# Transposing q and k together, splitting them in transposed form, and leaving two heads' probabilities unsplit

## The chip, the core and the metric

The kernel runs on one core of one Trainium2 chip. The core has a matrix engine (PE), a vector engine (VectorE, DVE in the rows), a scalar engine (ScalarE, ACT), a general engine (GpSimd, POOL) and a queue that issues transfers (SyncE, SP). Each runs its own instructions in the order written and waits for others by semaphores. PE multiplies a stationary operand, which it loads first (PEld), with a moving one, and writes to PSUM; the others work on on-chip memory, SBUF, and all but GpSimd also on PSUM. The metric is the time of one execution on the device, in microseconds.

## The reference

Two batches of eight heads attend over 768 positions of 64 features, and a position sees only those that fall in its hash bucket. The 1536 rows that come out go through two gated networks.

```python
q_bits = (np.einsum('bhsd,dk->bhsk', q, proj) > 0)     # 6 bits
k_bits = (np.einsum('bhsd,dk->bhsk', k, proj) > 0)
mask = q_bucket[:, :, :, None] == k_bucket[:, :, None, :]
scores = scale * np.matmul(q, k.transpose(0, 1, 3, 2))
scores = np.where(mask, scores, -1000000000.0)
attn = np.exp(scores - np.max(scores, axis=-1, keepdims=True))
attn = attn / (np.sum(attn, axis=-1, keepdims=True) + 1e-09)
return np.matmul(attn, v)
...
h = (x @ w1) * (x @ w2) @ w3                            # first network, then @ w_out
gate = 1.0 / (1.0 + np.exp(-(x @ w_gate)))              # second network
return (gate * (x @ w_val) @ w_out2)
```

The networks' weights come as 64-bit floats.

## The kernel before, in words

**Split operands.** A matmul takes its operands as float32r, a shortened float32 that PE runs in one pass. To keep precision a value is split in two such tiles, a high half (the value copied into float32r) and a low half (the value less its high half), and a product is summed from two or three matmuls. A transpose is a matmul with an identity as moving operand: `idf` in float32, `idr` in float32r.

**Heads.** `load_head` loads q, k and v of a head. `split` makes the split tiles `spq`, `spk`, `spv`: VectorE for heads 0 and 1 (of v only the high half), GpSimd for the later ones. `prep(h)` readies a head: 6 transposes of the split q and 6 of the split k, three into a PSUM tile `trr`; ScalarE copies these to `aq` and `ak` (64 rows of high half, 64 of low half, times 768); the hash `gps` multiplies `aq` and `ak` with the split projection `pq` in 8 matmuls of 384 columns; VectorE turns the signs into large numbers `ft`, which add to the scores what a mismatch costs. Five copies on SP bring the halves into the rows where the score matmul wants them. `first_head` does this for head 0 without those copies.

**Steps.** A head has six steps of 128 query rows, 96 in all. In one, `emit_qk` runs 4 score matmuls of 384 columns into one of two PSUM tiles, VectorE takes the maximum (L479) and a scale (L480), ScalarE the exponential with its sum (L490), PE transposes the probabilities `e` in 6 float32 transposes (L523), ScalarE copies them out as the high half (L526), VectorE writes the low half (L527). For each pair of steps `emit_av` multiplies them with the split v: 6 blocks of 128 keys, each with the high and the low half, 12 matmuls of 256 columns (L540). The stationary operand is the 64 columns of v's high half beside the 64 of its low half, so the result has 128 rows, of which `emit_x` adds the two halves.

**Beside it** runs a filler: 64-bit weights are decoded (`decode`, two ScalarE, one GpSimd and three VectorE instructions each), and w3 and w_out are multiplied into one matrix (`wacc`). From about step 52 the filler is the first network's first chunk of tokens (`gen_first`). After the last head come the networks for the rest (`moe`).

**The order** on each engine is worked out by `order_engines`: it takes all instructions of the attention part with their dependencies and priorities (by step; the preparation of a head 300 earlier), plays them against estimated costs, always starting the ready instruction of the smallest number on a free engine, and ties each engine to the order so found. Its cost of a PE instruction is `n / 2.4` ns for n columns, doubled for a float32 transpose, plus 2.5; of a GpSimd one `60 + n * 2.3`.

Of the kernel before, what the change touches and what calls it, by code (L numbers as in the profile page):

```python
# [228 lines left out]
def lsh_attention_moe_moe2_kernel(  # L229
# [132 lines left out]
    def split(h, nm, part):  # L362
        if not 0 <= h < NH:
            return
        if part == 0:
            t = ap_.tile([P, NT, 2, D], F32R, tag="sp" + nm, name=f"sp{nm}{h}", bufs=2 if nm == "v" else 1)
            splits[h, nm] = t
            (pool if h >= 2 else dve).tensor_copy(t[:, :, 0, :], raws[h, nm])
        else:
            t = splits[h, nm]  # L370
            (dve if h < 2 and nm != "v" else pool).tensor_tensor(out=t[:, :, 1, :], in0=raws[h, nm], in1=f(t[:, :, 0, :]), op=ALU.subtract)

    def alloc_mats(h):
# [4 lines left out]
        mats[h] = m

    def prep(h):  # L380

        load_head(h, "v")
        if h < NH:
            alloc_mats(h)
            m = mats[h]
            for nm, d in (("q", "aq"), ("k", "ak")):
                t = splits[h, nm]
                for half in range(2):
                    ps = psT.tile([P, 512], F32R, tag="t", name="trr")
                    for c in range(3):  # L390
                        pe.transpose(ps[:, c * P:(c + 1) * P], t[:, half * 3 + c].rearrange("p a d -> p (a d)"), idr)  # L391
                    act.activation(out=m[d][:, half * HS:(half + 1) * HS], in_=f(ps[:, :HS]), func=AF.Copy,
                                   scale=SCALE if nm == "q" else 1.0)
                    if nm == "q" and half == 1:
                        sync.dma_start(out=f(m["bq"][0:D]), in_=f(m["aq"][0:D]))
                    yield
            sync.dma_start(out=f(m["bk"][0:D]), in_=f(m["ak"][D:P]))
            for half in range(2):
                hs = slice(half * HS, (half + 1) * HS)
                ps = psT.tile([P, 512], F32, tag="t", name="gps")  # L400
                for n, nm in enumerate(("aq", "ak")):
                    for x in range(2):
                        pe.matmul(ps[:, :HS], lhsT=pq[n][x], rhs=m[nm][:, hs], start=n + x == 0, stop=n + x == 2)  # L403
                dve.tensor_scalar(out=m["ft"][:, hs], in0=ps[:, :HS], scalar1=thr[:, 0:1], scalar2=thr[:, 1:2],
# [11 lines left out]
        split(h - 1, "v", 0)
        split(h - 1, "v", 1)

    def first_head():
# [4 lines left out]
        kt = m["ft"]  # L424
        kps = []
        for nm, d in (("q", m["aq"]), ("k", kt)):
            t = splits[0, nm]
            for half in range(2):
                ps = psT.tile([P, 512], F32R, tag="t", name="trr")
                for c in range(3):  # L430
                    pe.transpose(ps[:, c * P:(c + 1) * P], t[:, half * 3 + c].rearrange("p a d -> p (a d)"), idr)
                kps = (kps + [ps])[-2:]
                act.activation(out=d[:, half * HS:(half + 1) * HS], in_=f(ps[:, :HS]), func=AF.Copy, scale=SCALE if nm == "q" else 1.0)
            if nm == "q":
                pool.tensor_copy(m["bq"][0:D], f(m["aq"][0:D]))
        for half in range(2):
            hs = slice(half * HS, (half + 1) * HS)
            act.activation(out=m["ak"][0:D, hs], in_=f(kps[half][0:D, :HS]), func=AF.Copy)
            dve.tensor_copy(m["ak"][D:P, hs], f(kps[half][0:D, :HS]))
        for half in range(2):  # L440
            act.activation(out=m["bk"][0:D, half * HS:(half + 1) * HS], in_=f(kps[half][D:P, :HS]), func=AF.Copy)
# [1 line left out]
        pss = []
        for half in range(2):
            hs = slice(half * HS, (half + 1) * HS)
            ps = psT.tile([P, 512], F32, tag="t", name="gps")
            pss.append(ps)
# [486 lines left out]
```

## Time and profile before

| | |
|---|---|
| median of 3 runs | 836.71 us (836.36 to 836.72) |
| the profiled execution | 834.55 us |
| its span, first to last instruction | 832.6 us |
| mean granted PE clock | 0.994 of full speed |
| busy: PE, VectorE, ScalarE, GpSimd | 801.0, 540.7, 523.9, 332.0 us |
| chain that ended last | PE 84%, VectorE 8%, ScalarE 5% |

A share of busy time is an average over stages with different limits: the attention part takes somewhat under the first half of the span, the networks the rest. A PE instruction is recorded from its start to its end, while the next starts before that, so PE's busy time says when PE had nothing at all, and the spacing of starts says what an instruction costs.

### The profile page before, as it was taken

What the parts mean: (1) busy time and instruction counts of PE and PEld (TensorE: products, weight loads), DVE (VectorE), ACT (ScalarE), POOL (GpSimd) and SP (SyncE); (2) the same over time, 40 slices, a digit from 0 to 9 for tenths busy, and PEclk for the clock granted to TensorE, in tenths of its full rate; (3) what the DMA queues carried; (4) which work ended last, traced back from release to release, by engine and by line L of the source; (5) the groups of instructions that cost most, each with busy time, mean ns of one, the idle gap of its engine ahead of it and who ended that gap; (6) DMA issues with size and microseconds to landing.
All of it is one profiled execution on the core that took longest, in us unless ns stands there. A gap on an engine that the chain in (4) does not pass through costs nothing.

```text
span 832.6 us, 12204 instructions
## 1 busy us (share of the span) xinstructions
PE 801.0 (96%) x4272; PEld 683.6 (82%) x4272; DVE 540.7 (65%) x969; ACT 523.9 (63%) x1024; POOL 332.0 (40%) x329
## 2 busy tenths in 40 slices
PE   6889989999989999999999999999999999999998
PEld 5767878888878989888888888888888888888886
DVE  7999998888799989988265545586752222222222
ACT  5888977777888998887345555756545333343332
POOL 3466332242355443328534343544443232333330
PEclk9999999999999999999999999999999999999999
DMA  7656554334245543412012122334301000010001
GB/s 236 172 162 170 155 159 134 103 87 130 64 133 136 138 121 99 125 45 77 0 34 94 55 73 93 110 104 150 102 1 51 1 1 1 1 51 1 0 1 50
DMA packets 44748, 71.15 MB, mean 85 GB/s; under 512 B 6096, under 2 KB 32720, under 8 KB 44688
## 3 DMA queue, kind: packets, MB, share of 16 engines
q1 hardware_dynamic: 44688, 70.39, 29.0%
q8 instruction: 33, 0.54, 0.3%
q14 instruction: 27, 0.22, 0.1%
HBM read 52.43 MB, written 3.19 MB: 67 GB/s over the span
## 4 chain that ended last, share of the span: by engine, by line
PE 84%; DVE 8%; ACT 5%; issue 1%; DMA 1%; POOL 0%; SPq 0%; ACTq 0%; DVEq 0%; POOLq 0%
PE m L701 17%; PE pb L701 17%; PE pa L701 17%; PE av L540 6%; PE tp L523 5%; PE p L701 5%; PE wacc L596 4%; PE s L469 3%; PE s L472 3%; PE y L701 3%; PE gps L403 2%; DVE pt L527 2%; DVE s L479 1%; PE trr L391 1%; ACT pt L526 1%
## 5 line engine op out<-in xcount | busy, mean ns | idle before, releaser
L741 DVE TENSOR_TENSOR pb<-pb,a 128x512 f32<-128x512 f32 x52 | 36.2, 698 | 147.1 <-PE pb L701 139.8
L523 PE MATMUL tp<-idf,e 128*128 128x128 f32 x576 | 102.9, 277 | 5.5 <-DVE pt L527 4.3
L490 ACT ACTIVATE e<-s,sm 128x768 f32<-128x768 f32 x96 | 95.8, 998 | 15.7 <-DVE sm L480 15.1
L527 DVE TENSOR_TENSOR pt<-tp,pt 128x384 fp32r<-128x384 f32 x192 | 101.2, 549 | 6.0 <-ACT pt L526 4.4
L336 POOL TENSOR_SCALAR da<-da 128x512 f32<-128x512 f32 x76 | 51.3, 676 | 133.0 <-ACT da L334 119.3
L526 ACT ACTIVATE pt<-tp 128x384 fp32r<-128x384 f32 x192 | 90.4, 494 | 21.4 <-PE tp L523 19.5
L701 PE MATMUL pa<-x,wah 128*128 128x512 f32 x320 | 99.0, 389 | 0.0
L479 DVE TENSOR_REDUCE s<-s 128x1 f32<-128x768 f32 x96 | 91.8, 956 | 11.0 <-PE s L472 10.7
L701 PE MATMUL pb<-x,wbh 128*128 128x512 f32 x320 | 98.5, 389 | 0.0
L695 POOL TENSOR_TENSOR wal<-xall,wah 128x512 fp32r<-128x512 f32 x36 | 47.4, 1317 | 110.2 <-ACT wah L276 109.6
L523 PEld LDWEIGHTS tp<-idf,e 128*128 128x128 f32 x576 | 72.0, 142 | 17.6 <-DVE pt L527 6.0
L540 PE MATMUL av<-pt,spv 128*128 128x256 f32 x576 | 78.7, 287 | 1.0 <-DVE pt L527 0.9
L334 ACT ACTIVATE da<-st 128x512 f32<-128x512 f32 x76 | 51.1, 672 | 42.7 <-DVE w1r L343 18.1
L540 PEld LDWEIGHTS av<-pt,spv 128*128 128x128 f32 x576 | 72.1, 191 | 4.2 <-DVE pt L527 1.3
L469 PE MATMUL s<-ak,aq 128*128 128x384 f32 x192 | 61.8, 386 | 10.7 <-ACT e L490 10.6
L701 PEld LDWEIGHTS pb<-x,wbh 128*128 128x128 f32 x320 | 60.1, 188 | 12.5
L701 PEld LDWEIGHTS pa<-x,wah 128*128 128x128 f32 x320 | 60.1, 188 | 12.5
L596 PE MATMUL wacc<-wo,t 128*128 128x512 f32 x192 | 65.3, 416 | 0.1
L701 PE MATMUL pa<-x,wal 128*128 128x512 f32 x160 | 62.3, 389 | 0.0
L701 PE MATMUL pb<-x,wbl 128*128 128x512 f32 x160 | 62.2, 389 | 0.0
L744 DVE TENSOR_TENSOR gl<-pb,gh 128x512 fp32r<-128x512 f32 x52 | 36.0, 691 | 40.0 <-ACT gh L276 40.0
L472 PE MATMUL s<-bk,bq 128*128 128x384 f32 x192 | 57.2, 359 | 0.3 <-DVE bq L453 0.3
(161 smaller groups left out, 1889.6 us busy)
## 6 DMA issues: line engine op xcount, KB each, us to landing
st<-in_moe_w_dram SPq DMA_DIRECT2D x32, 512.0 KB, 3.8
st<-in_moe_w_out_dram SPq DMA_DIRECT2D x20, 512.0 KB, 3.4
st<-in_moe_w_gate_dram SPq DMA_DIRECT2D x12, 512.0 KB, 3.5
st<-in_moe_w_val_dram SPq DMA_DIRECT2D x12, 512.0 KB, 3.5
rawq<-in_q_dram SPq DMA_DIRECT2D x16, 192.0 KB, 3.4
rawk<-in_k_dram SPq DMA_DIRECT2D x16, 192.0 KB, 3.2
rawv<-in_v_dram SPq DMA_DIRECT2D x16, 192.0 KB, 3.1
rr<-row SPq DMA_DIRECT2D x16, 192.0 KB, 3.3
```

The lines of the kernel that those rows point to most:

```text
L334: act.activation(out=f(a), in_=f(hw), func=AF.Abs)
L336: pool.tensor_scalar(out=f(a), in0=f(a), scalar1=F64_HI, scalar2=F64_LO, op0=ALU.min, op1=ALU.max)
L469: pe.matmul(s[:, half, :HS], lhsT=m["aq"][:, qs], rhs=m["ak"][:, ks], start=True, stop=False)
L472: pe.matmul(s[:, half, :HS], lhsT=m["bq"][:, qs], rhs=m["bk"][:, ks], start=False, stop=True)
L479: dve.tensor_reduce(out=one[:, 1:2], in_=s[:, :, :HS], op=ALU.max, axis=AX.XY, negate=True)
L490: act.activation(out=e.rearrange("p (a c) -> p a c", a=2), in_=s[:, :, :HS], func=AF.Exp, bias=sm[:, 1:2], scale=sm[:, 0:1], accum_out=su_ ...
L523: pe.transpose(ps[:, j * P:(j + 1) * P], e[:, c * P:(c + 1) * P], idf)
L526: act.activation(out=dh, in_=src, func=AF.Copy)
L527: dve.tensor_tensor(out=lo[:, g % 2, half * 3:half * 3 + 3], in0=src, in1=f(dh), op=ALU.subtract)
L540: pe.matmul(acc[:, :2 * P].rearrange("p (a t) -> p a t", a=2), lhsT=w, rhs=r[:, :, c], start=(c == 0 and i == 0), stop=(c == NT - 1 and i ...
L596: pe.matmul(acc, lhsT=t3[x][:, j], rhs=wo[y][:, j], start=(j == 0 and n == 0), stop=(j == NF1 - 1 and n == 2))
L701: mm = pe.matmul(ps, lhsT=lhs[x], rhs=rhs[y], start=start and n == 0, stop=stop and n == 2)
```

## The change

q and k of a head are joined side by side in float32 (`join`; q is scaled there), and one set of 6 float32 transposes turns both: 64 rows of q over 64 of k. ScalarE copies this out whole (`rt`), and the split follows in transposed form: GpSimd casts it into `aq` and subtracts into `bq`. The hash takes three matmuls for a half in place of four: high with high, low with high, high with low, q and k in one. The rows are brought in place by six copies instead of five. In the first two heads (`PLAIN`) the transposed probabilities stay one float32 tile, v is used as loaded, and a product has 6 matmuls on 64 columns of v; VectorE's L527 and L550 fall away there. The two halves of the score product change places. The planner's cost of a PE instruction gets a case of four passes for float32 operands with other than 128 columns.

```diff
-            return n / 2.4 * (2 if n == 128 and "float32r" not in str(rd[0].dtype) else 1) + 2.5
+            passes = 1 if "float32r" in str(rd[0].dtype) else 2 if n == 128 else 4
+            return n / 2.4 * passes + 2.5
...
-            (pool if h >= 2 else dve).tensor_copy(t[:, :, 0, :], raws[h, nm])
-        else:
-            t = splits[h, nm]
-            (dve if h < 2 and nm != "v" else pool).tensor_tensor(out=t[:, :, 1, :], in0=raws[h, nm], in1=f(t[:, :, 0, :]), op=ALU.subtract)
+        raws[h] = t = ap_.tile([P, NT, 2, D], F32, tag="qk", name=f"qk{h}", bufs=1)
+        eng = pool if h else dve
+        eng.tensor_scalar(out=t[:, :, 0, :], in0=raws[h, "q"], scalar1=0.0, scalar2=SCALE, op0=ALU.add, op1=ALU.mult)
+        eng.tensor_copy(t[:, :, 1, :], raws[h, "k"])
...
+    def both(h, half):
+        ps = psT.tile([P, 512], F32, tag="t", name="trr")
+        for c in range(3):
+            pe.transpose(ps[:, c * P:(c + 1) * P], raws[h][:, half * 3 + c].rearrange("p a d -> p (a d)"), idf)
+        return ps[:, :HS]
+    def hashes(m, half):
+        hs = slice(half * HS, (half + 1) * HS)
+        ps = psT.tile([P, 512], F32, tag="t", name="gps")
+        for n, (w, x) in enumerate(((0, "aq"), (0, "bq"), (1, "aq"))):
+            pe.matmul(ps[:, :HS], lhsT=pq[w], rhs=m[x][:, hs], start=n == 0, stop=n == 2)
+        return ps
...
             for half in range(2):
                 hs = slice(half * HS, (half + 1) * HS)
+                act_copy(t[:, hs], both(h, half))
+                pool.tensor_copy(m["aq"][:, hs], t[:, hs])
+                pool.tensor_tensor(out=m["bq"][:, hs], in0=t[:, hs], in1=f(m["aq"][:, hs]), op=ALU.subtract)
+                yield
+            for d in ("ak", "bk"):
+                sync.dma_start(out=f(m[d][0:D]), in_=f(m["aq"][D:P]))
+            sync.dma_start(out=f(m["bk"][D:P]), in_=f(m["bq"][D:P]))
...
+            sync.dma_start(out=f(m["bq"][D:P]), in_=f(m["aq"][0:D]))
+            sync.dma_start(out=f(m["ak"][D:P]), in_=f(m["ft"][0:D]))
+            sync.dma_start(out=f(m["aq"][D:P]), in_=f(m["ft"][D:P]))
             yield
...
-            pt_t[g // 2] = [ap_.tile([P, 2, NT, P], F32R, tag=f"pt{i}", name=f"pt{i}_{g}") for i in range(2)]
+            n, dt = (1, F32) if g < PLAIN * NT else (2, F32R)
+            pt_t[g // 2] = [ap_.tile([P, 2, NT, P], dt, tag=f"pt{i}", name=f"pt{i}_{g}") for i in range(n)]
...
         act.activation(out=dh, in_=src, func=AF.Copy)
-        dve.tensor_tensor(out=lo[:, g % 2, half * 3:half * 3 + 3], in0=src, in1=f(dh), op=ALU.subtract)
+        for d in dl:
+            dve.tensor_tensor(out=d, in0=src, in1=f(dh), op=ALU.subtract)
...
-        act_copy(x, acc[D:P, :2 * P])
-        dve.tensor_tensor(out=x, in0=acc[0:D, :2 * P], in1=x, op=ALU.add)
+        if h < PLAIN:
+            act_copy(x, acc[0:D, :2 * P])
+        else:
+            act_copy(x, acc[D:P, :2 * P])
+            dve.tensor_tensor(out=x, in0=acc[0:D, :2 * P], in1=x, op=ALU.add)
```

The planner's order, at three places. A number behind a name counts buffers; in `e2` or `sm3` the first number is the step, in `spq2` or `aq2` the head.

VectorE in head 0, steps 1 to 5, before (`pt1` is the low half, `da` and `wor` are decoded weights):

```order
L527 TENSOR_TENSOR pt1_0_322<-tp1_344,pt0_0_321 128x384
L527 TENSOR_TENSOR pt1_0_322<-tp1_350,pt0_0_321 128x384
L480 SCALAR_TENSOR_TENSOR sm3_339<-lim_77,s1_84 128x2
L343 ISA wor0_264<-da_370,dr_371 128x1024
L527 TENSOR_TENSOR pt1_2_386<-tp2_387,pt0_2_385 128x384
L527 TENSOR_TENSOR pt1_2_386<-tp2_393,pt0_2_385 128x384
L584 TENSOR_TENSOR t31_0_299<-w3t0_360,t30_0_298 128x512
L479 TENSOR_REDUCE s0_83<-s0_83 128x1
L479 TENSOR_REDUCE s1_84<-s1_84 128x1
L480 SCALAR_TENSOR_TENSOR sm4_380<-lim_77,s0_83 128x2
L527 TENSOR_TENSOR pt1_2_386<-tp3_433,pt0_2_385 128x384
L527 TENSOR_TENSOR pt1_2_386<-tp3_439,pt0_2_385 128x384
```

and now:

```order
L479 TENSOR_REDUCE s0_80<-s0_80 128x1
L338 SCALAR_TENSOR_TENSOR da_255<-st_239,da_255 128x512
L337 TENSOR_SCALAR da_330<-da_330 128x512
L343 ISA w3f_90<-da_255,dr_256 128x1024
L338 SCALAR_TENSOR_TENSOR da_330<-st_241,da_330 128x512
L480 SCALAR_TENSOR_TENSOR sm4_340<-lim_74,s0_80 128x2
L479 TENSOR_REDUCE s1_81<-s1_81 128x1
L343 ISA wor0_229<-da_330,dr_331 128x1024
L480 SCALAR_TENSOR_TENSOR sm5_382<-lim_74,s1_81 128x2
L337 TENSOR_SCALAR da_437<-da_437 128x512
L338 SCALAR_TENSOR_TENSOR da_437<-st_243,da_437 128x512
L343 ISA wor1_230<-da_437,dr_438 128x1024
```

The six low-half rows are gone, and decoding stands where they stood.

PE around the first product of head 0 and the preparation of head 2, before:

```order
L523 MATMUL tp2_393<-idf_69,e2_319 128x128 x3
L391 MATMUL trr_410<-idr_70,spq2_237 128x128 x3
L391 MATMUL trr_415<-idr_70,spq2_237 128x128 x3
L469 MATMUL s1_84<-ak0_135,aq0_133 128x384 x2
L472 MATMUL s1_84<-bk0_136,bq0_134 128x384 x2
L523 MATMUL tp3_433<-idf_69,e3_342 128x128 x3
L523 MATMUL tp3_439<-idf_69,e3_342 128x128 x3
L540 MATMUL av0_445<-pt0_0_321,spv0_247 128x256
L540 MATMUL av0_445<-pt1_0_322,spv0_247 128x256
L540 MATMUL av0_445<-pt0_0_321,spv0_247 128x256
L540 MATMUL av0_445<-pt1_0_322,spv0_247 128x256
L540 MATMUL av0_445<-pt0_0_321,spv0_247 128x256
```

and now (`av0` is the product, `gps` the hash):

```order
L394 MATMUL trr_368<-idf_69,qk2_208 128x128 x3
L523 MATMUL tp2_351<-idf_69,e2_284 128x128 x2
L584 MATMUL w3t0_320<-idf_69,w3f_90 128x128 x3
L394 MATMUL trr_375<-idf_69,qk2_208 128x128 x3
L523 MATMUL tp3_394<-idf_69,e3_304 128x128 x3
L523 MATMUL tp3_399<-idf_69,e3_304 128x128 x3
L541 MATMUL av0_404<-pt0_0_286,spv0_122 64x256 x6
L402 MATMUL gps_419<-aq2_362,pq0_71 128x384
L402 MATMUL gps_419<-bq2_363,pq0_71 128x384
L402 MATMUL gps_419<-aq2_362,pq1_72 128x384
```

One row of six unsplit matmuls stands for twelve, and the hash, which reads the cast `aq2` and the difference `bq2`, now follows the product.

GpSimd in the preparation of heads 2 and 3, before:

```order
L368 CAST spq2_237<-rawq2_189 128x6x64
L371 TENSOR_TENSOR spq2_237<-rawq2_189,spq2_237 128x6x64
L368 CAST spk2_240<-rawk2_191 128x6x64
L371 TENSOR_TENSOR spk2_240<-rawk2_191,spk2_240 128x6x64
L336 TENSOR_SCALAR da_370<-da_370 128x512
L336 TENSOR_SCALAR da_479<-da_479 128x512
L371 TENSOR_TENSOR spv1_664<-rawv1_193,spv1_664 128x6x64
L368 CAST spq3_654<-rawq3_243 128x6x64
L591 TENSOR_TENSOR wo1_92<-wor0_264,wo0_91 128x512
L371 TENSOR_TENSOR spq3_654<-rawq3_243,spq3_654 128x6x64
```

and now:

```order
L374 TENSOR_SCALAR qk2_208<-rawq2_166 128x6x64
L375 COPY qk2_208<-rawk2_168 128x6x64
L336 TENSOR_SCALAR da_255<-da_255 128x512
L336 TENSOR_SCALAR da_330<-da_330 128x512
L336 TENSOR_SCALAR da_437<-da_437 128x512
L417 CAST aq2_362<-rt2_367 128x384
L418 TENSOR_TENSOR bq2_363<-rt2_367,aq2_362 128x384
L417 CAST aq2_362<-rt2_367 128x384
L418 TENSOR_TENSOR bq2_363<-rt2_367,aq2_362 128x384
L374 TENSOR_SCALAR qk3_468<-rawq3_211 128x6x64
L375 COPY qk3_468<-rawk3_213 128x6x64
```

The split rows that read loaded data become rows that read `rt`, the transposed pair, with the two joining rows of the next head behind them.

## Rows read from the trace of the kernel before

**Rows 1.** The page's forty equal slices, PE and VectorE, busy tenths in order of time.
```profile
PE   6889989999989999999999999999999999999998
DVE  7999998888799989988265545586752222222222
```

**Rows 2.** Busy us by engine (instructions) in four stages, clock, DMA share, GB/s.
```profile
14.00:83.00 69.00, 58.86 (x373) 50.72 (x372) 66.52 (x124) 60.18 (x126) 40.73 (x44) 0.95 0.64 176
83.00:215.00 132.00, 125.78 (x836) 111.84 (x836) 117.02 (x222) 102.19 (x215) 40.54 (x49) 1.00 0.45 122
250.00:385.00 135.00, 134.76 (x883) 120.31 (x884) 119.90 (x237) 115.06 (x244) 56.85 (x62) 1.00 0.42 114
385.00:832.60 447.60, 443.79 (x1958) 367.18 (x1957) 196.55 (x296) 210.75 (x367) 170.56 (x145) 1.00 0.14 45
```

**Rows 3.** The chain of waits within 14 to 83 us, its shares by line.
```profile
by line: DVE pt L527 16.7%; issue 8.9%; DVE da L338 8.3%; DVE s L479 7.9%; DVE wor L343 5.7%; ACT pt L526 5.4%; DMA st<-in_moe_w_dram 4.6%; ACT wo L276 4.3%; PE gps L403 4.1%; ACT e L490 3.6%; ACT da L334 2.9%; DVE da L337 2.6%; DVE sm L480
```

**Rows 4.** Groups of instructions in 14 to 83 us: count, busy us, mean ns, idle before.
```profile
L527 DVE TENSOR_TENSOR pt<-tp,pt 128x384 fp32r<-128x384 f32 x34 | 18.2, 548 | 1.4 <-ACT pt L526 1.2
L550 DVE TENSOR_TENSOR xall<-av,xall 64x256 f32<-64x256 f32 x7 | 2.9, 413 | 0.1
L371 DVE TENSOR_TENSOR spk<-rawk,spk 128x384 fp32r<-128x384 f32 x1 | 0.6, 555 | 0.0
L368 DVE CAST spv<-rawv 128x384 fp32r<-128x384 f32 x1 | 0.4, 357 | 0.0
L392 ACT ACTIVATE ak<-trr 128x384 fp32r<-128x384 f32 x8 | 3.7, 495 | 0.1
L392 ACT ACTIVATE aq<-trr 128x384 fp32r<-128x384 f32 x8 | 3.6, 492 | 0.5 <-PE trr L391 0.5
L523 PE MATMUL tp<-idf,e 128*128 128x128 f32 x106 | 18.9, 284 | 2.0 <-DVE pt L527 1.7 <-DVE xall L550 0.2
L368 POOL CAST spq<-rawq 128x384 fp32r<-128x384 f32 x4 | 3.4, 844 | 8.9 <-PE trr L391 4.7 <-DMA rawq<-in_q_dram 4.2
```

**Rows 5.** The chain of waits within 222 to 240 us: start, us, what, then its last piece.
```profile
222.35 1.38 PE av L540 x12
223.73 0.21 PE trr L391 x3
228.13 0.69 PE gps L403 x4
228.82 0.33 PE tp L523 x3
229.15 0.36 PE s L472 x2
...
823.35 5.45 PE m L701 x24
```

**Rows 6.** Busy us by engine in a busy stretch of heads 1 to 3.
```profile
60.00:100.00 40.00, 37.35 (x250) 32.13 (x249) 39.65 (x77) 36.42 (x77) 21.20 (x24) 1.00 0.60 165
```

**Rows 7.** Groups of GpSimd instructions over the whole run.
```profile
L371 POOL TENSOR_TENSOR spq<-rawq,spq 128x384 fp32r<-128x384 f32 x14 | 16.1, 1152 | 1.0
L368 POOL CAST spq<-rawq 128x384 fp32r<-128x384 f32 x14 | 9.8, 697 | 12.4 <-PE trr L391 8.2 <-DMA rawq<-in_q_dram 4.2
```

**Rows 8.** Instructions in order of time around the start: start, us, what, idle before.
```profile
13.65 0.22 DVE L480 SCALAR_TENSOR_TENSOR sm<-lim,s 128x2 f32<-128x2 f32 x1
13.96 0.99 ACT L490 ACTIVATE e<-s,sm 128x768 f32<-128x768 f32 x1 [2.29 <-DVE sm L480]
21.14 0.46 SPq L410 DMA_DIRECT2D ak<-ak  x1
22.30 0.99 ACT L490 ACTIVATE e<-s,sm 128x768 f32<-128x768 f32 x1
34.12 0.51 PE L469 MATMUL s<-ak,aq 128*128 128x384 f32 x2
```

More of the change, by code (lines that the diff above doesn't have):

```diff
@@ L287, in lsh_attention_moe_moe2_kernel @@
     idf = cst.tile([P, P], F32, name="idf")
-    idr = cst.tile([P, P], F32R, name="idr")
     pq_raw = cst.tile([P, NB], F32, name="pq_raw")
-    pq = [[cst.tile([P, P], F32R, name=f"pq{a}{i}") for i in range(2)] for a in "qk"]
+    pq = [cst.tile([P, P], F32R, name=f"pq{i}") for i in range(2)]
     thr = cst.tile([P, 2], F32, name="thr")
@@ L385, in prep @@
             m = mats[h]
[L386 to L397, printed above, removed]
+            t = ap_.tile([P, S], F32, tag="rt", name=f"rt{h}", bufs=1)
             for half in range(2):
                 hs = slice(half * HS, (half + 1) * HS)
[L400 to L404, printed above, removed]
+                act_copy(t[:, hs], both(h, half))
[5 more added lines that the diff above has]
+            sync.dma_start(out=f(m["bk"][D:P]), in_=f(m["bq"][D:P]))
+            for half in range(2):
+                hs = slice(half * HS, (half + 1) * HS)
+                dve.tensor_scalar(out=m["ft"][:, hs], in0=hashes(m, half)[:, :HS], scalar1=thr[:, 0:1], scalar2=thr[:, 1:2],
                                   op0=ALU.is_gt, op1=ALU.mult)
@@ L423, in first_head @@
         m = mats[0]
[L424 to L435, printed above, removed]
@@ L436, in first_head @@
         for half in range(2):
             hs = slice(half * HS, (half + 1) * HS)
[L438 to L441, printed above, removed]
-        load_head(1, "qk")
[L443 to L447, printed above, removed]
-            for n, d in enumerate((m["aq"], kt)):
-                for x in range(2):
-                    pe.matmul(ps[:, :HS], lhsT=pq[n][x], rhs=d[:, hs], start=n + x == 0, stop=n + x == 2)
@@ L451, in first_head @@
-        for d, r in ((m["bk"], slice(0, D)), (m["bq"], slice(D, P))):
+            ps = both(0, half)
+            act_copy(m["aq"][:, hs], ps)
+            dve.tensor_tensor(out=m["bq"][:, hs], in0=ps, in1=f(m["aq"][:, hs]), op=ALU.subtract)
+            act_copy(m["ak"][0:D, hs], ps[D:P])
+            act_copy(m["bk"][0:D, hs], ps[D:P])
+        load_head(1, "qk")
+        dve.tensor_copy(m["bk"][D:P], f(m["bq"][D:P]))
+        pss = [hashes(m, half) for half in range(2)]
+        act_copy(m["bq"][D:P], f(m["aq"][0:D]))
@@ L452, in first_head @@
+        for d, r in (("ak", slice(0, D)), ("aq", slice(D, P))):
             for half in range(2):
-                dve.tensor_scalar(out=d[D:P, half * HS:(half + 1) * HS], in0=pss[half][r, :HS], scalar1=thr[r, 0:1], scalar2=thr[r, 1:2],
+                dve.tensor_scalar(out=m[d][D:P, half * HS:(half + 1) * HS], in0=pss[half][r, :HS], scalar1=thr[r, 0:1], scalar2=thr[r, 1:2],
                                   op0=ALU.is_gt, op1=ALU.mult)
-        for nm in "qk":
-            split(1, nm, 0)
-            split(1, nm, 1)
+        join(1)
@@ L537, in emit_av @@
         for c in range(NT):
-            w = sv[:, c].rearrange("p a d -> p (a d)")
-            for i, r in enumerate((hi, lo)):
-                pe.matmul(acc[:, :2 * P].rearrange("p (a t) -> p a t", a=2), lhsT=w, rhs=r[:, :, c],
-                          start=(c == 0 and i == 0), stop=(c == NT - 1 and i == 1))
+            w = sv[:, c]
+            for i, r in enumerate(pts):
+                pe.matmul(acc[:w.shape[1], :2 * P].rearrange("p (a t) -> p a t", a=2), lhsT=w, rhs=r[:, :, c],
+                          start=(c == 0 and i == 0), stop=(c == NT - 1 and i == len(pts) - 1))
     def emit_x(u):
@@ L826, in lsh_attention_moe_moe2_kernel @@
     dve.memset(thr[D + o:P, 0:1], -TINY)
-    for nm in "qk":
-        split(0, nm, 0)
-        split(0, nm, 1)
+    join(0)
     first_head()
```

58 lines of the change are left out of this document (28 added, 30 removed).

## The prediction

> **What bounds the kernel now.** I read the page's forty slices first, then the busy time of each engine by stage, then the chain of waits of the one stage in which the change takes most away. The slices [rows 1] show two halves. VectorE stands at seven to nine tenths in the first nineteen slices, at nine in slices 2 to 6 while PE has eight or nine; then it falls as far as two, and PE stays at nine. The stages say the same in us [rows 2]. 0 to 14 is the start, up to the first softmax tile. 14 to 83 is heads 0 to 2: VectorE is busy 66.52 of 69.00 us (96%), ScalarE 60.18 (87%), PE 58.86, GpSimd 40.73. From 250 to 385 PE is busy 134.76 of 135.00 us, and from 385 to the end 443.79 of 447.60. Nothing after 385 is touched, so that stretch moves as a block.
>
> The chain of waits in 14 to 83 [rows 3] names the same engine: its largest piece, 16.7% of the window or 11.5 us, is VectorE at L527, which writes the low half of the transposed probabilities. There are 34 of these in the window [rows 4], and 24 belong to heads 0 and 1.
>
> **The change, part by part.** The sum has four terms: the start, heads 0 to 2, the later heads, the MoE stages (0).
>
> *Heads 0 and 1 without the split of the probabilities.* VectorE loses in 14 to 83: 24 instructions of L527 at 548 ns, 13.2 us; 6 of the 7 additions of L550 at 413 ns, 2.5 us; one subtraction of head 1's k, 0.56 us, and one copy of a v tile, 0.36 us [rows 4]. That is 16.6 us, and 66.5 becomes 49.9: VectorE is no longer the bound there. The order printed for VectorE above shows how it looks: the low-half rows are gone and the decoding of weights stands closer together. ScalarE loses half of its copies out of the q and k transposes, since q and k now come out of one transpose: 8 of 16, 7.3 us in all [rows 4], so 3.65 us. 60.2 becomes 56.5.
>
> PE gains work. In these two heads 6 products of 6 matmuls each take unsplit float32 operands with 256 columns, in place of 12 matmuls each at 1.38 us for 12, 115 ns apart [rows 5]. No row shows such a matmul. The lower end is the split kind's spacing, 115 ns: then the half as many cost 36 x 115 less than now, -4.1 us. The nearest row of a float32 operand is the probability transpose, 3 in 0.33 us, 110 ns for 128 columns, so 220 ns for 256 [rows 5]. The upper end is four such passes, 880 ns. The changed planner prices it at four passes of the split kind: 256 / 2.4 x 4 + 2.5 = 429 ns. I take 429 because it lies nearer to the transpose row than to the upper end, and keep 115 and 880 for the range. The step on PE is then 6 x (2.57 - 1.38) = 7.1 us. With the hash's saving below, twice 173 ns for each of four heads prepared in this window (1.4 us), and a few tenths off the transposes, 58.9 becomes 64.1 us of PE busy time. That busy time overstates the array: a transpose is recorded for 284 ns [rows 4] and followed by the next after 110 [rows 5].
>
> What is late next is ScalarE with 56.5 us, PE close behind. The best share that ScalarE holds in a busy stretch of this stage is 36.42 of 40.00, 91% [rows 6]; its share over the stage is 87%. At 91% the stage would take 62.1 us, at 87.5%, which it has already, 64.6. I take 64.6, since PE at 64.1 busy leaves little room under it: 4.4 us less than 69.0. Both bounds stay: no gain if the stage is kept up by latencies and by the order written into it, and 10.8 us if ScalarE reaches 97%, as VectorE does now.
>
> *The preparation of the later heads.* For a head PE now runs 12 transposes, 3 in 0.21 us, so 0.84 us, and 8 hash matmuls, 4 in 0.69 us, so 1.38 us [rows 5]. Afterwards it runs 6 transposes of float32 operands at 110 ns, 0.66 us, and 6 hash matmuls, 1.04 us. That is 0.52 us less; for the 11 heads prepared after 83 us, 5.7 us. In 83 to 385 PE is the fullest engine [rows 2], so it counts there, but not in full, because the split of q and k now stands inside the chain. Before, GpSimd split them ahead of the transposes, from data long loaded. Now ScalarE copies the transposed pair out, GpSimd casts it and subtracts, and only then may the hash run. The piece of PE's order for head 2 shows it: the transposes, a block of probability transposes, the product of head 0, then the hash. GpSimd's cast of q took 697 ns, its subtraction 1152 [rows 7]; one half is 1.85 us, with the copy of 0.46 (3.65 us for 8) [rows 4] and three handovers of 0.1 us, as from the end of a scale (13.65 + 0.22) to exp 0 [rows 8], 2.6 us. In head 15 the order puts between the first half's transposes and the hash that reads the difference 3 transposes, 6 probability transposes, 12 product matmuls, 3 matmuls of 512 columns, 2 score matmuls and the hash's first: 0.33 + 0.66 + 1.38 + 0.68 + 0.36 + 0.17 = 3.6 us [rows 5]. It is covered, with 1.0 us to spare. ScalarE's queue can eat that: an exponential of 0.99 us [rows 8] may stand ahead of the copy. I count half of 5.7: 2.9 us. The bounds are 5.7 gained and the loss in the second rival.
>
> GpSimd has for each head two joining copies, two casts and two subtractions in place of two casts and two subtractions, so two more operations of about a cast's 0.7 us, 1.4 us, beside a load of 30 to 60% [rows 2]; it hides behind the other engines except in that chain. A head's SBUF copies become six for five; they hide behind the head before, since head 1's last copy is issued at 21.14 and its first scores run at 34.12 [rows 8]. On SP's queue the two early copies wait for GpSimd instead of ScalarE; queued behind them are the next q and k loads and the weight loads, which are issued well ahead. The score matmuls' halves change places at equal cost.
>
> The Trainium skill, page "SBUF — State Buffer", section "Who interferes with whom", says that VectorE in its two-port mode and GpSimd share a port pair as an exclusive lock, and that whichever comes second stands still for the other's whole instruction. It speaks against moving the split behind the transposes, on GpSimd. The trace leans that way: in 14 to 83, with VectorE at 96%, the cast of q took 844 ns against 697 over the whole run [rows 4, 7].
>
> *The start.* Exp 0 begins at 13.96 us, exp 1 only at 22.30 [rows 8], because head 1's preparation stands between them on VectorE. Of the start's chain the split goes and three ScalarE copies and one cast for each half come, in about the same time. I put +0.5 us, between -1 and +2; what follows sooner (exp 1) is inside the stage's 4.4.
>
> *The sum.* +0.5 - 4.4 - 2.9 - 0 = -6.8 us. The profiled execution took 834.55 us (832.6 of span and 1.95 around it), so it would be 827.75. The median of the timed runs is 2.16 us above the profiled one; 829.9, say 830.
>
> **The rivals.**
> *More comes back.* ScalarE reaches 97% in heads 0 to 2 (-10.8) and the later heads get all of 5.7: -16.0, 820.7. For it: VectorE does hold 96%. Against it: PE's 64.1 us.
> *The hash waits for GpSimd: slower.* PE works in order, so a hash matmul whose operand is late stops the scores, transposes and products behind it, and ScalarE and VectorE starve. The spare is 1.0 us, or none behind an exponential. If one cast and one subtraction each lose a VectorE instruction of 0.55 us, the length of L527 [rows 4], each of 14 heads loses 1.1 us: +15.4 - 6.8 = +8.6, 845.3. It decides from (6.8 + 1.7) / 14 = 0.6 us a head. For it: 844 against 697 ns. Against it: the second half's order leaves the chain room.
> *Plain float32 costs 880 ns: slower.* PE's busy time in 14 to 83 goes to 64.1 + 36 x 0.451 = 80.3 us, 11.3 over the stage's 69: +11.3 - 2.9 + 0.5 = +8.9, 845.6. It decides from about 680 ns. For it: only that no row excludes it. The Trainium skill, page "TensorE: Matmul & The Clock Gate", section "Terms", says that transpose mode makes float32 four times faster; by that a plain product would cost four times its transpose, this case. No row here shows it.
> *The relief is lost.* VectorE's time in heads 0 to 2 was a queue and not the limit, and the stage stays 69: +0.5 - 2.9, 834.3. For it: exp 1's 8 us behind exp 0 is an order, not a load. Against it: L527 is 11.5 us of the chain.
>
> **How the numbers follow.** Forecast 0.55 (823 to 834), more 0.12, lost relief 0.15, late hash 0.10, dear float32 0.08. A measurement of this kernel can tell about 0.2%, 1.7 us, from no change: 835.0 to 838.4. Faster: 0.55 + 0.12 + half of 0.15, 0.74. Same: the other half and milder forms of the two slower cases, 0.12. Slower: 0.14. The range 821 to 839 leaves out the far ends of three rivals.
>
> **What would show it.** Right: heads 0 to 2 take 64 to 65 us instead of 69, VectorE there is near 50 us busy, ScalarE at 87% or more; the plain product takes 2.4 to 2.8 us for six; PE waits at the hash for GpSimd less than 0.5 us a head; 14 ends within a us of where it does. Wrong: the plain product over 4 us, long PE waits on the GpSimd cast or subtraction, or a stage of 69 us with every engine under 85%.

## The result, and the profile after

The changed kernel takes 825.32 us (median; 824.83 to 825.83) beside 836.54 us for the kernel before in the same rounds: a ratio of 0.9871, 95% interval 0.9856 to 0.9887, so 11.2 us or 1.3% less. Forecast were 830.0 us and a range of 821 to 839; that range also holds 836.5, the time without any change, so the terms tell more than the number. The profiled execution took 824.83 us with a span of 823.0, which is 9.6 us of span less than before; the terms below are of these two executions.

Three rows of the page's forty slices answer to [rows 1]: PE, VectorE and the granted clock.
```profile
PE   6898999999999999999999999999999999999998
DVE  7869989888799989988175545686642222322222
PEclk9999999999999999999999999999999999999999
```
VectorE is lower in slices 2, 3 and 6 (8, 6 and 8 where 9 stood in each), and in slices 3 and 6 PE is the fuller engine. The windows of the profile after (columns as in [rows 2]) give it in us: heads 0 to 2, which now end at 78, and the heads from head 7 to the last exponential.
```profile
14.00:78.00 64.00, 58.44 (x332) 44.46 (x332) 52.58 (x92) 54.77 (x116) 40.49 (x49) 1.00 0.69 193
169.38:360.50 191.12, 184.72 (x1187) 161.97 (x1186) 173.60 (x338) 155.02 (x328) 89.09 (x104) 1.00 0.45 122
```
The kernel before took from the same instruction to the same instruction:
```profile
176.28:368.80 192.52, 187.56 (x1240) 167.99 (x1239) 172.03 (x334) 159.61 (x341) 76.44 (x86) 0.99 0.42 113
```
In the first row VectorE is busy 52.58 of 64.00 us, 82%, where it stood at 96% [rows 2]; PE is at 91%, ScalarE at 86%. The other two rows show the later heads: PE is busy 2.84 us less, the stretch is 1.40 us shorter, so PE stands idle 6.40 us in it where it was 4.96.

The timeline of the profile after (start, us, what, idle before and what ended it) answers to [rows 8]:
```profile
14.59 0.99 ACT L490 ACTIVATE e<-s,sm 128x768 f32<-128x768 f32 x1 [0.39 <-PE gps L402]
15.58 0.98 ACT L490 ACTIVATE e<-s,sm 128x768 f32<-128x768 f32 x1
34.52 2.80 PE L541 MATMUL av<-pt,spv 128*64 128x256 f32 x12
78.32 0.99 ACT L490 ACTIVATE e<-s,sm 128x768 f32<-128x768 f32 x1 [0.16 <-DVE sm L480]
169.38 0.99 ACT L490 ACTIVATE e<-s,sm 128x768 f32<-128x768 f32 x1
```
These are exps 0 and 1, one plain product, and the first exps of heads 3 and 7. Exp 1 runs 1.0 us behind exp 0, where it was 8.3 us behind. Heads 0 to 2 take 78.32 - 14.59 = 63.7 us. Before, head 3's first exp was this one, so they took 83.47 - 13.96 = 69.5 us:
```profile
83.47 0.99 ACT L490 ACTIVATE e<-s,sm 128x768 f32<-128x768 f32 x1 [0.72 <-DVE sm L480]
```
The plain product's 6 matmuls stand as 12 records, 2.80 us from the first start to the last end. The next matmul starts before that end, and as a piece of the chain of waits, which is how [rows 5] has the split product's 1.38 us, the plain one takes 2.73: +1.35 for each of six, +8.1 us, on an engine that is now the fullest of the stage. The chain of waits within 14 to 78, beside [rows 3], with one of its pieces:
```profile
by line: PE av L541 19.7%; DVE s L479 11.6%; PE tp L523 9.0%; DVE da L338 7.2%; DMA bk<-aq 6.6%; issue 6.5%; PE wacc L600 4.8%; PE gps L402 4.8%; DVE pt L528 4.2%; PE s L469 4.1%; DVE w3f L343 3.9%; PE s L472 3.6%; DVE da L337 3.2%; PE trr 
34.59 2.73 PE av L541 x12
```
VectorE's L527 is gone (the low half is L528 now, 4.2%). The largest share is the product on PE, 19.7% or 12.6 us: four of the plain ones and, with 1.68 us, a split one of head 2. Behind it stands VectorE's maximum over the scores, L479.

**By terms.** Start: +0.6 us (exp 0 at 13.96, then 14.59). Heads 0 to 2: -5.8. The other heads: -3.1 (285.3 us from exp 18 to exp 95, then 282.2). After the last exponential: -1.3 (463.8, then 462.5). Sum -9.6. The medians differ by 11.2; the profiled execution of before was 2.0 us below its median, the one of after 0.5 below.

### The profile page after: what moved, and what is told of

It is laid out like the page before. It is cut to its first block, busy times and chain, and to the rows that moved or that the text cites. A ratio compares the mean times of both kernels' runs of the same rounds, so it can differ in the third digit from the quotient of the medians.

```text
span 823.0 us, 11970 instructions
## 1 busy us (share of the span) xinstructions
PE 795.7 (97%) x4144; PEld 667.9 (81%) x4144; DVE 523.7 (64%) x929; ACT 511.1 (62%) x993; POOL 347.6 (42%) x360
## 4 chain that ended last, share of the span: by engine, by line
PE 83%; DVE 9%; ACT 2%; DMA 2%; POOL 2%; issue 1%; SPq 0%; POOLq 0%; DVEq 0%; ACTq 0%
PE pa L705 17%; PE m L705 17%; PE pb L705 17%; PE av L541 7%; PE tp L523 5%; PE wacc L600 4%; PE p L705 4%; PE s L469 3%; PE s L472 3%; DVE s L479 3%; PE y L705 2%; PE gps L402 2%; DVE pt L528 2%; DVE da L338 1%; PE trr L394 1%
## 5 line engine op out<-in xcount | busy, mean ns | idle before, releaser
L526 ACT ACTIVATE pt<-tp 128x384 fp32r<-128x384 f32 (+1 forms) x192 | 89.9, 493 | 19.8 <-PE tp L523 17.4
L479 DVE TENSOR_REDUCE s<-s 128x1 f32<-128x768 f32 x96 | 91.1, 954 | 11.6 <-PE s L472 10.4
L528 DVE TENSOR_TENSOR pt<-tp,pt 128x384 fp32r<-128x384 f32 x168 | 87.8, 547 | 4.1 <-ACT pt L526 2.9
L541 PE MATMUL av<-pt,spv 128*128 128x256 f32 (+1 forms) x576 | 85.1, 297 | 1.7 <-DVE pt L528 1.4
L541 PEld LDWEIGHTS av<-pt,spv 128*128 128x128 f32 (+1 forms) x576 | 72.6, 182 | 11.1 <-DVE pt L528 2.4
L469 PE MATMUL s<-bk,bq 128*128 128x384 f32 x192 | 61.9, 384 | 6.3 <-ACT e L490 6.0
L338 DVE SCALAR_TENSOR_TENSOR da<-st,da 128x512 uint32<-128x512 uint32 x76 | 58.5, 771 | 1.2
```

The lines of the kernel that those rows point to most:

```text
L338: dve.scalar_tensor_tensor(out=a, in0=hw, scalar=0xC0000000, in1=a, op0=ALU.bitwise_and, op1=ALU.bitwise_or)
L469: pe.matmul(s[:, half, :HS], lhsT=m["bq"][:, qs], rhs=m["bk"][:, ks], start=True, stop=False)
L479: dve.tensor_reduce(out=one[:, 1:2], in_=s[:, :, :HS], op=ALU.max, axis=AX.XY, negate=True)
L526: act.activation(out=dh, in_=src, func=AF.Copy)
L528: dve.tensor_tensor(out=d, in0=src, in1=f(dh), op=ALU.subtract)
L541: pe.matmul(acc[:w.shape[1], :2 * P].rearrange("p (a t) -> p a t", a=2), lhsT=w, rhs=r[:, :, c], start=(c == 0 and i == 0), stop=(c == NT ...
```

## The experiments

The program orders its instructions with a planner that puts a price on each, so every edit also changes the order. For that reason the parts were run alone, together and under a second order. One number carries most of what follows, the start of the 43rd exponential, head 7's first: the time up to there is the early part, and from there to the end of the span the late part. All are read from each run's trace as above. Head 3's start is a worse mark, since the filler done by then differs from run to run: it is 78.74 in e10 and 75.67 in e3, beside 78.32 in after, while head 7 starts at 175.70, 169.50 and 169.38. The ratio is to the kernel before in the same rounds.

| run | what it is | median, ratio (95%) | exp 1 behind exp 0 | early part | late part |
|---|---|---|---|---|---|
| before | | 836.54 | 8.3 | 176.28 | 656.3 |
| after | joint transposes, 2 plain heads | 825.32, 0.9871 (0.9856-0.9887) | 1.0 | 169.38 | 653.6 |
| e1 | joint transposes alone | 831.11, 0.9946 (0.9928-0.9964) | 4.9 | 175.78 | 653.5 |
| e2 | 2 plain heads alone | 835.80, 0.9994 (0.9978-1.0011) | 9.1 | 176.74 | 656.7 |
| e3 | after, 3 plain heads | 825.07, 0.9874 (0.9847-0.9900) | 1.0 | 169.50 | 653.6 |
| e4 | after, old price of plain float32 | 838.09, 1.0022 (1.0006-1.0038) | 1.0 | 179.12 | 653.4 |
| e5 | before, GpSimd price 1.8 | 841.42, 1.0068 (1.0045-1.0091) | 8.2 | 179.81 | 661.8 |
| e6 | after, GpSimd price 1.8 | 826.97, 0.9892 (0.9870-0.9914) | 1.0 | 168.00 | 657.2 |
| e7 | e1, GpSimd price 1.8 | 832.76, 0.9957 (0.9943-0.9972) | 5.8 | 173.45 | 656.8 |
| e8 | e2, GpSimd price 1.8 | 838.32, 1.0029 (1.0010-1.0048) | 8.1 | 175.14 | 662.3 |
| e9 | e2, head 1's q and k split on GpSimd | 829.15, 0.9909 (0.9893-0.9925) | 1.0 | 170.25 | 656.9 |
| e10 | after, head 1's q and k on VectorE | 831.10, 0.9932 (0.9916-0.9948) | 6.9 | 175.70 | 653.4 |
| e11 | after, GpSimd price 1.8 then 2.3 | 823.48, 0.9848 (0.9822-0.9873) | 1.0 | 168.18 | 653.7 |
| e12 | after, a 4th hash matmul from head 4 | 830.08, 0.9924 (0.9903-0.9945) | 1.0 | 169.72 | 657.9 |

**Each part alone (e1, e2).** e1 is the changed kernel with `PLAIN = 0`: every head's probabilities are split.
```diff
-    PLAIN = 2
+    PLAIN = 0
```


> The changed kernel with the first two heads split like the others (PLAIN = 0): joint transposes and three-pass hash alone. Theory V (most of the gain is VectorE's work taken out of heads 0 to 2, the later heads give about 3 us): 831 to 834 us, with heads 0 to 2 at 67 to 69 us again and VectorE over 93% busy there. Rival P (the cheaper preparation of the heads gives nearly all): 825 to 828 us. Rival O (the planner happened on a better order): no fixed time, but heads 3 to 15 change by 3 us or more against the changed kernel although their work is the same.

e2 is the kernel before with the two plain heads and the price that goes with them; q and k are prepared in the old way.
```diff
-                t = ap_.tile([P, NT, D], F32, tag="raw" + nm, name=f"raw{nm}{h}", bufs=1)
+                if nm == "v" and h < PLAIN:
+                    t = ap_.tile([P, 2, NT, D], F32, tag="spv", name=f"spv{h}")[:, 0]
...
-        dve.tensor_tensor(out=lo[:, g % 2, half * 3:half * 3 + 3], in0=src, in1=f(dh), op=ALU.subtract)
+        for d in dl:
+            dve.tensor_tensor(out=d, in0=src, in1=f(dh), op=ALU.subtract)
```


> The kernel before, with only the unsplit probabilities and v in heads 0 and 1 (and the planner's price for them). V: heads 0 to 2 lose 4 to 6 us, nothing else moves: 830.5 to 832.5 us. P: 835 to 837 us. If V and P both hold in part, the gains of this run and of the one without unsplit heads add up to the 11.2 us of both together within 2 us; under O they do not.

e1 took 831.11 us, e2 835.80. The late part follows the preparation alone: 653.5 with the joint transposes, 656.7 without. The early part does not add up: plain heads alone +0.5, joint transposes alone -0.5, both -6.9. Yet e2 did take the load off VectorE, as its row for 14 to 83 us shows, with 56.03 us beside 66.52 [rows 2]:
```profile
14.00:83.00 69.00, 61.86 (x346) 48.85 (x346) 56.03 (x91) 57.35 (x122) 37.60 (x41) 0.93 0.60 170
```
Ten us less on VectorE, bought with the plain products' 8.1 us more on PE, brought nothing here. So e1's time lies in the range of theory V and e2's in that of P, and neither theory holds for both.

**A third plain head (e3), the planner's price (e4).** e3 is after with `PLAIN = 3`. e4 is after with the line of before that prices a plain float32 product like one pass, 109 ns.
```diff
-            passes = 1 if "float32r" in str(rd[0].dtype) else 2 if n == 128 else 4
-            return n / 2.4 * passes + 2.5
+            return n / 2.4 * (2 if n == 128 and "float32r" not in str(rd[0].dtype) else 1) + 2.5
```


> The changed kernel with three unsplit heads. V: VectorE loses 7.8 us more (12 subtractions of 0.55 and 3 additions of 0.41), PE gains 3 x 1.4 = 4.3 us in a stretch in which it has about 5 us free: 823 to 826 us, no clear difference from two. P: PE is what counts, so its 4.3 us are lost: 828 to 830 us.

> The changed kernel, planned with the old price of a PE instruction, so that the unsplit product of 2.8 us is planned as 0.65 us. V: the loads are the same and so is the time within 2 us: 824 to 828 us. O (the order makes the gain): 829 us or more, with PE's waiting in heads 0 and 1 grown by as much.

e3 took 825.07 us, no more than after. In its chain of waits for 14 to 83 us PE's product leads by far:
```profile
by line: PE av L541 31.7%; PE tp L523 16.9%; PE s L469 10.8%; PE s L472 9.4%; PE wacc L600 8.4%; PE gps L402 6.8%; DVE s L479 5.5%; PE trr L394 3.5%; ACT e L490 1.5%; PE w3t L584 1.4%; issue 1.1%; DVE w3f L343 1.0%; DVE t L588 0.9%; DVE da 
```
e4 lost all the gain: 838.09 us, 12.8 more than after. Its profiled execution, its shortest with 834.33 us, has 9.7 of it before head 7 (179.12 beside 169.38) and the same late part. It runs the same instructions in another order. Its row for 14 to 83 us has every engine lower than [rows 2] but PE:
```profile
14.00:83.00 69.00, 59.74 (x331) 44.44 (x331) 46.82 (x85) 52.06 (x111) 37.21 (x47) 1.00 0.59 160
```
and waits there (engine, line, what it waited for: us, times, longest) have grown behind the product that the planner believed short:
```profile
ACT xall L276 <- PE av L540: 9.4, 6, 1.8
DVE s L478 <- PE s L471: 8.1, 3, 3.2
```
The first comes to 0.6 us in the same window of after. From exp 0 to head 7 PE stands idle 17.7 us in e4 (busy 147.07 of 164.77) and 11.4 in after (143.43 of 154.79).

**A second order (e5 to e8).** Is the sum of parts above an accident of one order? The planner's price for GpSimd is put at 1.8 ns an element for all four kernels.
```diff
-            return 60 + n * 2.3
+            return 60 + n * 1.8
```


> The kernel before, same work, planned with GpSimd at 60 + 1.8 n ns in place of 2.3 n (nearer to its recorded 0.7 us for 384 columns): another order of the same instructions. Theory L (load decides: the order is only noise of 1 us): 835 to 837 us. Theory O (the order decides what heads 0 to 5 take): off by 2 us or more either way in heads 0 to 5.

> The changed kernel, planned with GpSimd at 60 + 1.8 n. L: 824 to 827 us. O: heads 0 to 5 differ by 2 us or more from the changed kernel's first order, in either direction; the heads after and the tail keep 3 to 4 us of gain over the kernel before.

> The changed kernel without unsplit heads (PLAIN = 0), planned with GpSimd at 60 + 1.8 n. L: 829.5 to 832.5 us as in the first order of it. O: off by 2 us or more in heads 0 to 5. In both: heads 6 to 15 and the tail as in the changed kernel, since joint preparation alone makes their gain.

> The kernel before with two unsplit heads alone, planned with GpSimd at 60 + 1.8 n. L (the first order of it was an unlucky draw, VectorE's 16.6 us are worth 3 to 6): 830 to 833 us. Theory J (the relief of VectorE pays only together with the joint preparation, because head 1's split on VectorE still parts the first two exponentials and leaves PE at half clock): 834 to 837 us, with exp 1 again 8 us behind exp 0 and a granted clock below 1 between 10 and 30 us.

Late part again by the preparation: 661.8 and 662.3 with the old one, 657.2 and 656.8 with the new. Early part: plain heads alone -4.7, joint transposes alone -6.4, both -11.8. So in this order each part pays for itself and in the early part the two add up, and it is not a law that the relief brings nothing. The ranges given for the times of e5 (835 to 837 us), e7 (829.5 to 832.5) and e8 (830 to 837) all missed. In both orders the plain heads on top of the joint transposes are worth the same in medians, 831.11 - 825.32 and 832.76 - 826.97, 5.8 us each.

**The order at exp 1 (e9, e10).** Under the price 2.3 the runs whose exp 1 comes 1.0 us behind exp 0 have the short early part, all but e4 with its other price of PE. Both runs move head 1's q and k work between VectorE and GpSimd and edit nothing else. e9 is e2 with it on GpSimd:
```diff
-            (pool if h >= 2 else dve).tensor_copy(t[:, :, 0, :], raws[h, nm])
+            (pool if h >= 1 else dve).tensor_copy(t[:, :, 0, :], raws[h, nm])
...
-            (dve if h < 2 and nm != "v" else pool).tensor_tensor(out=t[:, :, 1, :], in0=raws[h, nm], in1=f(t[:, :, 0, :]), op=ALU.subtract)
+            (dve if h < 1 and nm != "v" else pool).tensor_tensor(out=t[:, :, 1, :], in0=raws[h, nm], in1=f(t[:, :, 0, :]), op=ALU.subtract)
```


> The kernel before with two unsplit heads, and head 1's q and k split on GpSimd instead of VectorE; the old preparation otherwise. Theory J (the relief is lost in the start, where head 1's split parts exp 0 and exp 1 and PE falls to half clock): exp 1 within 2 us of exp 0, granted clock near 1 from 10 to 30 us, head 7 begins 4 to 6 us earlier than with two unsplit heads alone (176.7 us), 829 to 832 us. Theory T (only the joint transposes, one chain less, let the relief through): 834 to 837 us.

e10 is after with it on VectorE:
```diff
-        eng = pool if h else dve
+        eng = pool if h > 1 else dve
...
+                eng = dve if h == 1 else pool
```


> The changed kernel with head 1's joining, cast and subtraction on VectorE instead of GpSimd, 3.0 us of VectorE work moved into the start. J: exp 1 falls 4 us or more behind exp 0, the clock dips between 10 and 30 us, 829 to 832 us. T: 824 to 827 us.

e9 took 829.15 us, 6.6 less than e2, and e10 831.10, 5.8 more than after; both differences lie in the early part (-6.5 and +6.3). VectorE's timeline shows why. In e2:
```profile
13.38 0.22 DVE L485 SCALAR_TENSOR_TENSOR sm<-lim,s 128x2 f32<-128x2 f32 x1
...
13.85 0.55 DVE L376 TENSOR_TENSOR spk<-rawk,spk 128x384 fp32r<-128x384 f32 x1
...
16.46 0.96 DVE L484 TENSOR_REDUCE s<-s 128x1 f32<-128x768 f32 x1
18.57 1.32 DVE L409 TENSOR_SCALAR ft<-gps,thr 128x384 fp32r<-128x384 f32 x2 [1.15 <-PE gps L408]
19.80 1.03 DVE L344 CUSTOM_DVE_ANT_0 w3f<-da,dr 128x1024 uint16<-128x1024 uint16 x1
21.50 0.69 DVE L593 TENSOR_TENSOR t<-w3t,t 128x512 fp32r<-128x512 f32 x1 [0.67 <-ACT t L277]
22.11 0.21 DVE L485 SCALAR_TENSOR_TENSOR sm<-lim,s 128x2 f32<-128x2 f32 x1
```
and in e9, without the decoding between, and with exps 0 and 1 from its ScalarE timeline:
```profile
11.55 1.83 DVE L484 TENSOR_REDUCE s<-s 128x1 f32<-128x768 f32 x2 [0.33 <-PE s L477]
13.41 0.22 DVE L485 SCALAR_TENSOR_TENSOR sm<-lim,s 128x2 f32<-128x2 f32 x1
13.66 0.99 ACT L495 ACTIVATE e<-s,sm 128x768 f32<-128x768 f32 x1 [0.38 <-DVE sm L485]
13.92 0.21 DVE L485 SCALAR_TENSOR_TENSOR sm<-lim,s 128x2 f32<-128x2 f32 x1
14.65 0.98 ACT L495 ACTIVATE e<-s,sm 128x768 f32<-128x768 f32 x1
```
Exp 1 needs the maximum of its scores (L484) and the small scale `sm` made of it (L485, 0.21 us). In e2 the maximum stands behind head 1's split, and the scale another 4.7 us later behind `ft`, which waits for PE's hash of head 1; exp 1 starts at 22.83. In e9 both maxima come first, as one group, and exp 1 follows exp 0. In e10 the second maximum is back at 14.66 and its scale at 20.52, behind head 1's cast, subtraction and `ft`:
```profile
14.66 0.95 DVE L480 TENSOR_REDUCE s<-s 128x1 f32<-128x768 f32 x1
...
16.66 1.32 DVE L419 TENSOR_TENSOR bq<-rt,aq 128x384 fp32r<-128x384 f32 x2
...
20.52 0.21 DVE L481 SCALAR_TENSOR_TENSOR sm<-lim,s 128x2 f32<-128x2 f32 x1
```
Neither run isolates exp 1's wait. Each also moves work between the engines (in e9 VectorE loses two casts and two subtractions, about 1.8 us), and the planner orders all that follows anew. Nor does e10 lose its time in heads 0 to 2, as these windows from exp 0 to exp 18 show, e10 first, then after:
```profile
14.37:78.74 64.37, 58.62 (x315) 44.31 (x314) 52.50 (x91) 53.48 (x114) 34.63 (x41) 0.96 0.64 178
14.59:78.32 63.73, 58.17 (x332) 44.41 (x333) 52.34 (x91) 54.73 (x115) 40.22 (x49) 1.00 0.69 192
```
By then e10 has 17 matmul records fewer behind it; head 3 has 160 of them for 120 and takes 25.6 us for 19.4, 6.2 of the 6.3 us. That a late exp 1 puts PE's work off, to be paid for before head 7, fits this, and is argued, not shown.

A rival was the clock: the granted clock between 10 and 30 us is 0.83 before, 0.74 in e2 and 1.00 after. e9 excludes it as the main cause:
```profile
10.00:30.00 20.00, 15.37 (x86) 13.59 (x85) 18.01 (x29) 15.38 (x33) 10.93 (x14) 0.83 0.79 246
```
The clock is that of before, and the gain is there; e4 has a clock of 1.00 in this stretch and no gain. Between e2 and e9 the clock rises by 0.09 of 20 us, which can be worth 1.8 of the 6.5 us at most. e10 has 0.91 there, and so have e3 and e11, which start head 7 at 169.50 and 168.18; e10 has 0.91 once more from 70 to 90 us, 1.8 us at most. That the clock would come near 1 with the early exp 1 was expected, and missed.

**Both prices in one program (e11).** Price 1.8 makes the early part of after 1.4 us shorter and the late part 3.6 longer. e11 takes 1.8 up to the 31st exponential in the program's order and 2.3 behind it.
```diff
+    marks = [j for j, i in enumerate(ins) if eng[j] == "Activation" and count(i.outs[0]) == 768]
+    cut = marks[30]
...
-            return 60 + n * 2.3
+            return 60 + n * (1.8 if k < cut else 2.3)
```


> The changed kernel, planned with GpSimd at 60 + 1.8 n up to the 31st exponential and 60 + 2.3 n after it. If heads 0 to 6 and the rest add up as the runs so far say (168.1 us to head 7 by the one price, 653.5 from there by the other), the span is 821.6 us and the time 822 to 825 us. If what is planned early only shifts work into later heads: 825 to 828 us.

823.48 us, parts of 168.2 and 653.7: the short one of each. It is 1.5% faster than the kernel before and has the shortest median of all runs; from after its interval (0.9822 to 0.9873 beside 0.9856 to 0.9887) does not separate it, only the spans, 821.9 and 823.0, point the same way.

**What PE's time is worth later (e12).** From head 4 on, each hash half gets a fourth matmul, low half by low half: 24 matmuls of 0.173 us [rows 5], 4.2 us of PE.
```diff
+        terms = ((0, "aq"), (0, "bq"), (1, "aq")) + (((1, "bq"),) if more else ())
...
+                dve.tensor_scalar(out=m["ft"][:, hs], in0=hashes(m, half, h >= 4)[:, :HS], scalar1=thr[:, 0:1], scalar2=thr[:, 1:2],
```


> The changed kernel with a fourth hash matmul for each half from head 4 on (low half times low half): 12 heads x 2 x 0.175 = 4.2 us more of PE work, nothing less. If a later head's PE work counts by half, as forecast: +2 us, 826.5 to 828.5. If it counts in full: 829 to 830.5. If it hides: 824.5 to 826.

The span grows by 4.6 us, the median by 4.8, and 4.3 us of the span's growth lie in the late part. That is what PE work that counts in full would cost. It isn't separated from two other things: the added matmuls also lengthen the chain from the hash to the scores, and the granted clock falls to 0.83 from 217 to 237 us, where after has 1.00.

## Why the prediction was right

**The start.** Forecast +0.5, measured +0.6.

**Heads 0 to 2: right in size, its reason true in one order only.** Forecast 69.0 to 64.6, measured 69.5 to 63.7. The step said that the stage gives way because VectorE's 16.6 us go, and that "what is late next is ScalarE" at a share of 87.5%. ScalarE's share came out at 86%, and the stage's time with it; since ScalarE was not what came next, that agreement is luck. And e2 has the same relief (VectorE 56.03 us in 14 to 83, after 57.41), but its early part is no shorter, while e8, under the second order, gains 4.7 us by it. What the step lacked is the order. The prediction had seen the 8 us between exp 0 and exp 1 and put them with the rival of the lost relief, as "an order, not a load", and counted them inside the stage's 4.4 as if they came by themselves. e9 shows that moving head 1's q and k work off VectorE, with the plain heads and without the joint transposes, brings exp 1 forward and the early part down by 6.5 us; e10 shows that after loses 6.3 with that work back on VectorE. In the changed kernel exp 1 comes early since head 1's join, cast and subtraction stand on GpSimd. An early exp 1 is not sufficient: e4 has it and starts head 7 9.7 us late. Nor is it the only way, since e8 gains 4.7 us with exp 1 8.1 behind. How much of the gain is owed to exp 1's wait itself was not measured.

**What is late next.** PE, not ScalarE: 91% busy in the stage, its product first in the chain, and e3, which relieves VectorE further and loads PE by half as much again, gains nothing by head 7. The term for the product was too small, 455 ns a matmul (2.73 us / 6) beside the 429 taken; 8.1 us of PE in place of 7.1. The 91% that the step took for ScalarE's best share in this stage [rows 6] is from 60 to 100 us, which runs 17 us past the stage.

**The later heads.** Forecast -2.9 as half of PE's 5.7, measured -3.1; e1 shows the late part moved by the preparation alone (-2.8; in the second order -5.0). The half was a guess, and why it came so close is in part open. From head 7 on, 1.44 of the 2.84 us stand as new idle time of PE. The step took PE as the fullest engine from 83 to 385 us, but [rows 2] leaves out 215 to 250. There VectorE is the fuller one: from 225 to 245 us before it is busy 19.20 of 20.00 and PE 15.83, and from 217 to 237 after 19.61 and 17.37. Work taken from PE need not shorten such a stretch. The granted clock in these two is 0.91 and 1.00, 1.8 us at most; e11 has 0.91 from 215 to 235, and its late part is that of after. The waits of PE from 169 to 361 us in the profile after, of which the second stood at none before:
```profile
PE s L469 <- ACT e L490: 2.9, 3, 1.6
PE tp L523 <- DVE pt L528: 1.8, 3, 1.3
```
PE's probability transposes wait for VectorE's low halves, 1.8 us, and not, as the step feared, the hash for GpSimd. VectorE is busy 173.60 of 191.12 us there.

**After the heads.** Forecast 0, measured -1.3. The last 381.3 us of both spans are alike (1666 matmul records, PE busy 377.40 and 377.49). The 1.3 us lie between the last exponential and there, 82.5 us before and 81.2 after, with 389 and 380 matmul records; PE is idle for 0.1 us of it before and not at all after. Whether nine matmuls moved ahead of the last exponential or records are missing stays open. With the 1.4 us more from heads 0 to 2 this is nearly all that the span lost beyond the forecast, 9.6 us for 6.8.

**The rivals.** The hash did not wait for GpSimd. The idle time of PE ahead of the hash matmuls, over the whole run of after:
```profile
  ACT aq L277: 1.7, 3
  POOL bq L418: 1.5, 2
```
1.5 us in 2 waits, where the rival needed 0.6 us a head. GpSimd's operations came out shorter than those the chain was priced with ([rows 7], 697 and 1152 ns):
```profile
L418 POOL TENSOR_TENSOR bq<-rt,aq 128x384 fp32r<-128x384 f32 x30 | 32.2, 1075 | 2.4
L417 POOL CAST aq<-rt 128x384 fp32r<-128x384 f32 x30 | 19.3, 643 | 6.1 <-ACT rt L277 5.9 <-PE s L472 0.2
```
The lock that the Trainium skill names ("SBUF — State Buffer", section "Who interferes with whom") is hidden in the mean of these two, but single casts fit it. Twenty of the 30 casts took 0.50 or 0.51 us, ten 0.69 to 1.04, and each of the ten ended 0.36 or 0.37 us after the end of an instruction of VectorE's decoding (L337, L338, L343). Two of them, and a short one for comparison:
```profile
93.70 0.76 DVE L343 CUSTOM_DVE_ANT_0 w3f<-da,dr 128x1024 uint16<-128x1024 uint16 x1
93.86 0.97 POOL L417 CAST aq<-rt 128x384 fp32r<-128x384 f32 x1
...
276.41 0.68 DVE L338 SCALAR_TENSOR_TENSOR da<-st,da 128x512 uint32<-128x512 uint32 x1
276.42 1.04 POOL L417 CAST aq<-rt 128x384 fp32r<-128x384 f32 x1 [0.15 <-PE s L472]
...
140.90 0.50 POOL L417 CAST aq<-rt 128x384 fp32r<-128x384 f32 x1
```
So the rival's mechanism occurs, with up to 0.5 us a cast in ten of 30, and the chain to the hash had room for it. The plain product at 880 ns fell with the 455 measured. By the Trainium skill ("TensorE: Matmul & The Clock Gate", section "Terms") it would have been four times its transpose; the trace has 2.1 times (455 for 220), and the measurement decides. More came back than forecast, 11.2 us of 16.0, but not by that rival's mechanism: ScalarE did not reach 97%. The lost relief is what e2 shows. With head 1's work on VectorE it would have come about in the changed kernel as well: e10 took 831.10 us, no less than e1 without plain heads (831.11), and kept the gain of the later heads.

## What to carry to other kernels

What load taken off the fullest engine is worth depends on the order: the same relief brought nothing in e2 and 4.7 us of the early part in e8. Where it brings nothing, look for one small instruction (here a 0.21 us scale) that stands in the queue behind long ones which wait themselves, and try moving those away (6.6 us in e9). Judge it at a mark up to which the runs have done the same work. Where a planner sets the order, a new kind of instruction needs a price near its measured time, or its order costs more than the change brings (12.8 us here). Measure the parts of a change alone, together and under a second order, since their sum depends on the order.

## What the runs showed of the hardware

A plain float32 matmul of 256 columns stands in the trace as two weight loads and two matmuls, and takes 455 ns at a granted clock of 1.00, four times the 115 ns of the split kind's [rows 5] and 2.1 times a float32 transpose for the same columns (110 ns for 128).

GpSimd's cast of 128x384 takes 0.50 us alone or beside VectorE's maximum, and up to 1.04 us beside VectorE's decoding; the long ones end 0.36 or 0.37 us after the VectorE instruction does.
